# Cosine attention ahead of a leaky-ReLU feed-forward: one PSUM store, score tiles in blocks of three, squares behind norm products, weights requested at other places

## Chip, cores and metric

The kernel runs on one core of a Trainium2 chip. The metric is device time of one execution in microseconds; lower is better. A core has five engines with instruction streams of their own: TensorE (PE, with weight loads shown apart as PEld), VectorE (DVE), ScalarE (ACT), GpSimd (POOL) and SyncE (SP). DMA requests are issued from SP, ACT and POOL and are carried by 16 DMA engines. Matrix products land in PSUM, which has 8 banks of 512 float32 columns on each of 128 partitions; SBUF is the larger working memory.

## What is computed

```python
def _attn_ref(q, k, v, tau):                 # 8 batches, 12 heads, 448 rows, 64 columns
    q_n = q / (np.linalg.norm(q, axis=-1, keepdims=True) + 1e-06)
    k_n = k / (np.linalg.norm(k, axis=-1, keepdims=True) + 1e-06)
    scores = np.matmul(q_n, k_n.transpose(0, 1, 3, 2)) / tau
    scores = scores - np.max(scores, axis=-1, keepdims=True)
    attn = np.exp(scores)
    attn = attn / (np.sum(attn, axis=-1, keepdims=True) + 1e-09)
    return np.matmul(attn, v).astype(np.float32)

def _moe_ref(x, w_in, w_out):                # 3584 rows, 768 -> 2048 -> 768
    h = x @ w_in
    g = np.maximum(0.01 * h, h)
    return (g @ w_out).astype(np.float32)
```

`x` is the attention's output with the heads side by side: 3584 rows (8 batches of 448) of 768 columns.

## The kernel before

**Slots.** Two heads of one batch form a slot `s`: 6 slots a batch (NPAIR), 48 in all. Two slots form a quad `j` of four heads: 3 a batch (NQ), 24 in all.

**Loads.** `load_qk(s)` issues four DMA requests on SP (q rows 0 to 383, k rows 0 to 383, and the last 64 rows of q and of k); four buffers, so slot s+4 is requested once slot s is normalised. `load_v(j)` issues one request on POOL, `load_v_rem(b)` four. The weights come through POOL too: `load_w_in(i)`, four pieces of 768 KB, `load_w_out(half)`, two of 1536 KB. POOL takes its instructions in order, so a request stands behind whatever POOL does before it.

**Norms of a slot.** `squares(s)` (L141: POOL, two products, q and k; the first three slots partly on ACT and DVE), `sums(s)` (L152: DVE, two reduces), `roots(s)` (L159 to L161: ACT, logarithm, exponential, addition), `normalise(s)` (L169 reciprocal and L173, the two "norm products" `qn`, DVE). `transposes(s)` then makes `qkT[s]`: up to slot 9 on TensorE with a DVE copy out of PSUM (L187, L208), from slot 10 on as a DMA transpose on SP (L202). `norms(s)` is roots, normalise, the DMA transpose and the loads of slot s+4. `hold(x)` is a copy of one column on POOL that reads `x`: what stands behind it on POOL does not start before `x` is written.

**Scores.** `scores(s, kis)` makes key tiles: for tile 0, 1 or 2 two matmuls of 64 contraction rows, side by side in the array (64x128, one for each head); tile 3 holds the last 64 keys of both slots of a quad and takes four matmuls of 64x64. Each key tile fills two PSUM banks, and one ACT exponential of 128x896 empties it (L238). All matmuls of one call are issued first, then its exponentials.

**Attention of a quad.** `totals(j)` sums the exponentials with a matrix of ones (16 matmuls of 128x32, four abreast) and takes the reciprocal on ACT as logarithm and exponential (L260, L261). `products(j, e)` multiplies with v (16 such matmuls for each of two halves `e`), `scale(j, e)` (L279, DVE) multiplies the result out of PSUM with the reciprocal into `xT`. `attend(j)` is all of it: 48 matmuls, 2 ACT, 2 DVE instructions. The text calls it the attention.

**Feed-forward.** Eight chunks `c` of 384 or 512 rows in turn. `first(c, m)`: 16 groups of 6 matmuls against w_in, each emptied by ACT as a leaky ReLU (L301, Prelu). `second(c, ts, half)`: groups of 16 matmuls against w_out, each emptied by a DVE copy (L331), then stored by SP. `work` lists the groups with a due place; `feed(place)` issues those that are due, `feed_groups(n)` the next n.

**PSUM.** Score tiles have a pool of two buffers of two banks (`p_sc`); all else (totals, values, transposes, both feed-forward products) rotates through four buffers of one bank (`p_mm`).

**Order.** The order of every engine is the order of the calls, written out by hand (`manual_schedule`). Opening: slots 0 to 5 in a loop (L440) with fill matmuls that keep TensorE busy. Then a stretch for slots 6 and 7, in which the first 13 w_in groups are issued. Then a loop over pairs of slots:

```python
        squares(s + 4)
        scores(s, (0, 1))
        attend(j)
        load_v(s // 2 + 1)
        scores(s, (2,))
        scores(s + 1, (0,))
        sums(s + 3)
        feed(s + 0.67)
        norms(s + 3)
        squares(s + 5)
        scores(s + 1, (1, 2))
        sums(s + 4)
        feed(s + 1.33)
        norms(s + 4)
        scores(s + 1, (3,))
        feed(s + 2)
```

In each batch's turn the chunk of the batch before is fed. After the last attention the rest of the feed-forward runs alone.

Of the kernel before, what the change touches and what calls it, by code (L numbers as in the profile page):

```python
# [8 lines left out]
F32 = mybir.dt.float32  # L9
# [7 lines left out]
def kernel(  # L17
# [27 lines left out]
    LATE = 0.3  # L45
    OPENING = 13
# [17 lines left out]
    scp = ctx.enter_context(tc.tile_pool(name="p_sc", bufs=2, space=PS))  # L64
    mmp = ctx.enter_context(tc.tile_pool(name="p_mm", bufs=4, space=PS))

    nc.scalar.preload_act_table_set("natural_log_exp_and_others")
    gp = nc.gpsimd

# [125 lines left out]

    def transposes(s):
        if s >= NSLOT:
            return
        dst = qtp.tile([128, 7, 128], BF16, name="qkT")
        qkT[s] = dst.rearrange("p t c -> p (t c)")  # L200
        if s >= DMA_FROM:
            nc.sync.dma_start(  # L202
                out=dst, in_=qn[s].rearrange("p t h d -> p (t h d)"), transpose=True
            )
            return
        tp = mmp.tile([128, 7, 128], BF16, name="tp", tag="mm")
        one(tp, s, 0, 7)
        nc.vector.tensor_copy(out=dst, in_=tp)  # L208
# [3 lines left out]
    def scores(s, kis):  # L212

        if s >= NSLOT:
            return
        tiles = []
        for ki in kis:
            sc = scp.tile([128, 2, 512], F32, name="sc")
# [11 lines left out]
        for ki, sc in zip(kis, tiles):  # L230
# [25 lines left out]
    def totals(j):  # L256
        sm = mmp.tile([128, 512], F32, name="sm", tag="mm")
# [8 lines left out]
    def products(j, e):  # L266
        b, jj = divmod(j, NQ)
        po = mmp.tile([128, 512], F32, name="po", tag="mm")
# [5 lines left out]
    def scale(j, e):  # L274
# [7 lines left out]
        )  # L282

# [5 lines left out]
    def first(c, m):  # L289
# [3 lines left out]
        pm = mmp.tile([128, 512], F32, name="pm", tag="mm")  # L293
# [22 lines left out]
    def second(c, ts, half):  # L316
        c0, n = chunk_cols(c)
        po2 = mmp.tile([128, 512], F32, name="po2", tag="mm")
# [29 lines left out]

    work = []
    for c in range(B):  # L350
        c0, n = chunk_cols(c)
        groups = [(6 * n, lambda c=c, m=m: first(c, m)) for m in range(MT)]
# [3 lines left out]
        groups += [  # L356
            (MT * HALF, lambda c=c, ts=ts, half=half: second(c, ts, half)) for ts, half in order
        ]
        total, done = sum(g[0] for g in groups), 0
        if c == 0:  # L360

            work += [(0, fn) for _, fn in groups[:OPENING]]
            groups = groups[OPENING:]
            total = sum(g[0] for g in groups)
        for cost, fn in groups:
            start = NPAIR * (c + 1) + (LATE if c else 2)
            end = NPAIR * (c + 2) + LATE
            work.append((start + (end - start) * (done + cost / 2) / total, fn))
            done += cost

    def feed(place):
        while work and work[0][0] <= place:
            work.pop(0)[1]()

    def feed_groups(count):
        for _ in range(count):
            work.pop(0)[1]()
# [23 lines left out]
    def fill(count):  # L401
        wm = mmp.tile([128, 512], F32, name="wm", tag="mm")
# [25 lines left out]
    for lo, hi, copy in ((0, 4, nc.scalar.copy), (4, 7, nc.vector.tensor_copy)):  # L428
        tp = mmp.tile([128, 7, 128], BF16, name="tp", tag="mm")
# [10 lines left out]
    for s in range(NPAIR):  # L440
# [16 lines left out]
        if s == 0:  # L457
            hold(qn[1][:, 6, 0, 0:1])
# [3 lines left out]
        if s < 4:  # L462
            load_w_in(s)
        if s == 4:
            load_w_out(0)
            load_v_rem(1)
# [19 lines left out]
    def attend(j):  # L486
        totals(j)
        for e in range(2):
            products(j, e)
# [10 lines left out]

    for s in range(NPAIR, NSLOT + 1, 2):
        j = s // 2 - 1
        if s == NPAIR:

            squares(s + 3)
            attend(j)
            scores(s, (0, 1))
            sums(s + 1)  # L510
            feed_groups(1)
            norms(s + 1)
            hold(qn[s + 1][:, 6, 0, 0:1])
            squares(s + 4)
            load_w_out(1)
            sums(s + 2)
            feed_groups(3)
            transposes(s + 1)
            roots(s + 2)
            feed_groups(2)  # L520
            scores(s, (2,))
            scores(s + 1, (0,))
            normalise(s + 2)
            load_qk(s + 6)
            hold(qn[s + 2][:, 6, 0, 0:1])
            load_v(s // 2 + 1)
            squares(s + 5)
            sums(s + 3)
            roots(s + 3)
            feed_groups(2)  # L530
            scores(s + 1, (1, 2))
            normalise(s + 3)
            load_qk(s + 7)
            feed_groups(1)
            transposes(s + 2)
            sums(s + 4)
            feed_groups(2)
            roots(s + 4)
            scores(s + 1, (3,))
            normalise(s + 4)  # L540
            transposes(s + 4)
            load_qk(s + 8)
            feed_groups(1)
            transposes(s + 3)
            feed_groups(1)
            continue
        squares(s + 4)
        scores(s, (0, 1))
        attend(j)
        if s >= NSLOT:  # L550
            break
        load_v(s // 2 + 1)
        scores(s, (2,))
        scores(s + 1, (0,))
        sums(s + 3)
        feed(s + 0.67)
        norms(s + 3)
        squares(s + 5)
        if (s + 2) % NPAIR == 0:
            load_v_rem(s // NPAIR + 1)  # L560
        scores(s + 1, (1, 2))
        sums(s + 4)
        feed(s + 1.33)
        norms(s + 4)
        scores(s + 1, (3,))
        feed(s + 2)
    feed(1e9)

# [34 lines left out]
```

## Time and profile before

| | us |
|---|---|
| median of 3 runs | 436.07 (435.71 to 436.48) |
| the profiled execution | 435.32 |
| its span, first to last instruction | 433.6 |
| granted TensorE clock over the span | 0.996 of full |
| TensorE busy, 0 to 42 us | 33.76 of 42.00 |
| TensorE busy, 61 to 382 us | 319.85 of 321.00 |
| one exponential of a score tile (L238) | 0.91 |
| one w_out request, issue to landing | 17.1 |
| one w_in request, issue to landing | 10.3 |

The profile was taken from one execution, and its times count from that execution's first instruction. A timeline line reads: start, length, engine, line of the code, operation, output and inputs by tile name, shape, number of instructions, and in brackets the idle time of the engine before it with what ended it. Matmul lengths overlap, since matmuls are pipelined and their ends are modelled; the step from one start to the next is the measured quantity. "128*32" behind a matmul is the part of the array in use, rows by columns.

### The profile page before, as it was taken

The page shows a single profiled execution, that of the slowest core. Times are in us where ns is not written, and L with a number is a line of the kernel's source. Part 1 is how long each engine was busy: PE and PEld are TensorE (multiplying, and loading weights), DVE is VectorE, ACT ScalarE, POOL GpSimd, SP SyncE. Part 2 cuts the span into 40 slices and gives each one's busy share as a digit, 9 for nine tenths or more (in the row PEclk, how much of TensorE's full clock was granted, in tenths as well). Part 3 has the DMA queues.
Part 4 walks back from the last instruction along what each step waited for, and adds up shares of the span by engine and source line. Part 5 has one row for each costly group of instructions (what it writes and reads, how often), then busy time and mean ns, then how long its engine had stood idle before and what let it go on. Part 6 is the DMA issues. An engine that isn't in the chain of part 4 may idle for free.

```text
span 433.6 us, 8498 instructions
## 1 busy us (share of the span) xinstructions
PE 418.9 (97%) x3305; PEld 206.0 (48%) x3319; DVE 189.3 (44%) x364; ACT 269.4 (62%) x496; POOL 129.6 (30%) x162
## 2 busy tenths in 40 slices
PE   8589999999999999999999999999999999999995
PEld 3134454544455555544455554544455555554563
DVE  5976755643335435632345444633436343220021
ACT  4897697488644788467753787557854587524300
POOL 4737642742161233341251213532232200000000
PEclk9999999999999999999999999999999999999999
DMA  8999999984468547766367555777185621010022
GB/s 169 187 223 255 212 219 183 167 200 114 82 115 178 109 113 141 135 142 140 45 149 142 125 136 105 129 178 143 23 173 119 101 58 23 36 74 2 0 74 73
DMA packets 104744, 54.11 MB, mean 125 GB/s; under 512 B 70784, under 2 KB 99712, under 8 KB 104704
## 3 DMA queue, kind: packets, MB, share of 16 engines
q1 hardware_dynamic: 79152, 41.44, 40.5%
q0 software_dynamic: 25056, 11.80, 22.0%
q8 instruction: 26, 0.43, 0.4%
q10 hardware_dynamic: 496, 0.33, 0.2%
q14 instruction: 14, 0.11, 0.1%
HBM read 45.61 MB, written 11.01 MB: 131 GB/s over the span
## 4 chain that ended last, share of the span: by engine, by line
PE 88%; DMA 6%; DVE 2%; ACT 1%; SPq 1%; issue 1%; POOL 0%; DVEq 0%; POOLq 0%
PE po L320 34%; PE pm L295 33%; PE sc L226 9%; PE po L249 8%; PE sm L249 4%; DMA q_h<-in_q_dram 4%; DVE qn L173 2%; DMA qkT<-qn 2%; ACT pe L238 1%; PE tp L187 0%; SPq L105 0%; SPq L102 0%; POOL sq L141 0%; DVE ss L152 0%; PE wm L404 0%
## 5 line engine op out<-in xcount | busy, mean ns | idle before, releaser
L238 ACT ACTIVATE pe<-sc 128x896 bf16<-128x896 f32 x144 | 123.6, 913 | 59.8 <-PE sc L226 57.3
L320 PE MATMUL po<-w_out_sb,hT 128*128 128x384 bf16 x896 | 151.9, 326 | 0.0
L295 PE MATMUL pm<-xT,w_in_sb 128*128 128x384 bf16 (+1 forms) x757 | 150.8, 352 | 0.9 <-issue 0.5
L320 PEld LDWEIGHTS <-hT 128*128 128x128 bf16 x896 | 84.8, 98 | 64.0 <-issue 10.4
L141 POOL TENSOR_TENSOR sq<-q_h 128x512 f32<-128x512 f32 x45 | 47.3, 1052 | 202.5 <-DMA q_h<-in_k_dram 153.5
L295 PEld LDWEIGHTS <-w_in_sb 128*128 128x128 bf16 x768 | 72.6, 98 | 74.1 <-issue 9.9
L301 ACT ACTIVATE hT<-pm 128x384 bf16<-128x384 f32 (+1 forms) x128 | 66.8, 545 | 51.5 <-PE pm L295 51.0
L331 DVE COPY osb<-po 128x384 f32<-128x384 f32 (+1 forms) x56 | 31.0, 554 | 91.6 <-PE po L320 87.5
L279 DVE TENSOR_TENSOR xT<-po,rb 128x448 bf16<-128x448 f32 x48 | 27.9, 619 | 70.6 <-ACT rb L261 70.6
L152 DVE TENSOR_REDUCE ss<-sq 128x8 f32<-128x512 f32 (+1 forms) x96 | 55.2, 610 | 2.1 <-ACT sq L139 1.1
L226 PE MATMUL sc<-qkT 64*128 64x448 bf16 (+1 forms) x384 | 50.5, 362 | 4.1 <-ACT pe L238 2.4
L169 DVE RECIPROCAL r<-ss 128x14 f32<-128x14 f32 x48 | 11.5, 239 | 66.7 <-ACT ss L161 66.7
L141 POOL TENSOR_TENSOR sq<-k_h 128x384 f32<-128x384 f32 x45 | 38.7, 859 | 0.0
L173 DVE TENSOR_TENSOR qn<-q_h,r 128x512 bf16<-128x512 f32 x48 | 36.0, 750 | 1.9 <-DVE r L169 0.3
L249 PE MATMUL po<-pe,v_b 128*32 128x448 bf16 x576 | 35.6, 353 | 0.0
L226 PEld LDWEIGHTS <-qkT 64*128 64x128 bf16 (+1 forms) x384 | 11.8, 96 | 40.6 <-issue 36.3
L173 DVE TENSOR_TENSOR qn<-k_h,r 128x384 bf16<-128x384 f32 x48 | 29.4, 612 | 0.0
L159 ACT ACTIVATE ss<-ss,tiny 128x14 f32<-128x14 f32 x48 | 14.6, 305 | 14.9 <-DVE ss L152 14.9
L238 ACT ACTIVATE pr<-sc 128x896 bf16<-128x896 f32 x24 | 21.7, 903 | 1.5 <-PE sc L226 1.5
L249 PEld LDWEIGHTS <-v_b 128*32 128x32 bf16 x576 | 15.2, 97 | 11.9 <-issue 0.4
L128 POOL DMA_DIRECT2D v_rem<-in_v_dram x32 | 20.4, 642 | 0.0
L120 POOL DMA_DIRECT2D v_b<-in_v_dram x24 | 19.3, 805 | 0.0
(39 smaller groups left out, 161.2 us busy)
## 6 DMA issues: line engine op xcount, KB each, us to landing
q_h<-in_q_dram SPq DMA_DIRECT2D x48, 192.0 KB, 3.2
k_h<-in_k_dram SPq DMA_DIRECT2D x47, 192.0 KB, 3.2
out_dram<-osb SPq DMA_DIRECT2D x30, 192.0 KB, 2.8
v_b<-in_v_dram POOLq DMA_DIRECT2D x24, 192.0 KB, 3.9
out_dram<-osb SPq DMA_DIRECT2D x12, 384.0 KB, 2.9
w_in_sb<-in_moe_w_in_dram POOLq DMA_DIRECT2D x4, 768.0 KB, 10.3
w_out_sb<-in_moe_w_out_dram POOLq DMA_DIRECT2D x2, 1536.0 KB, 17.1
q_h<-in_q_dram SPq DMA_DIRECT2D x48, 32.0 KB, 3.2
```

Of the source, the lines that this page charges most:

```text
L128: gp.dma_start(out=vrb[b % 2][lo : lo + 64, :, g], in_=r[g])
L141: eng.tensor_tensor(sq, x, x, op=ALU.mult)
L152: nc.vector.tensor_reduce(o.rearrange("p (h t) -> p h t", h=2), sqs[s][i], axis=AX.X, op=ALU.add)
L173: nc.vector.tensor_tensor(qn[s][:, lo:hi], x.rearrange("p h t d -> p t h d"), r[:, r0 : r0 + 2 * nt].rearrange("p (h t) -> p t h", h=2) .u ...
L226: nc.tensor.matmul(out=out[:, a, :S], lhsT=x[rows, c0:c1], rhs=x[rows, 0:S], start=True, stop=True,)
L238: nc.scalar.activation(out=dst, in_=sc[:, :, :S], func=AF.Exp, scale=inv_tau)
L249: nc.tensor.matmul(out=x[32 * g : 32 * g + 32, :S], lhsT=weights(g, ki) if ki < 3 else rem(g), rhs=pe[s][:, ki, a, :] if ki < 3 else pr[j] ...
L279: nc.vector.tensor_tensor(xT[m][:, 2 * jj + e, half * S : (half + 1) * S], pos.pop((j, e))[:, :S], rbs[j], op=ALU.mult,)
L295: nc.tensor.matmul(out=pm[:, :n], lhsT=w_in_sb[:, kt, m * 128 : (m + 1) * 128], rhs=xT[c // 2][:, kt, c0 : c0 + n], start=(kt == 0), stop= ...
L301: nc.scalar.activation(out=hT[c][:, m, :n], in_=pm[:, :n], func=AF.Prelu, alpha=0.01)
L320: nc.tensor.matmul(out=po2[:, :HALF], lhsT=hT[c][:, m, ts * 128 : (ts + 1) * 128], rhs=w_out_sb[:, m, half * HALF : (half + 1) * HALF], st ...
L331: nc.vector.tensor_copy(out=o[:, half * HALF : half * HALF + cut], in_=po2[:, :cut])
```

## The change

Five things are changed.

1. The two PSUM pools become one tile `ps` of all eight banks. `banks(count)` hands out one bank, or two that start at an even bank, those that were used longest ago; `kept` keeps value banks of the opening out of it until they are scaled. In the opening (`deals["apart"]`) two-bank tiles come from banks 0 to 3 and single ones from 4 to 7, afterwards all from all.
2. From batch 1 on, the loop over pairs of slots becomes a list of units: seven a batch (`whole`), five in batch 1 (`opened`). A unit is an optional attention, then a block of two or three key tiles (all their matmuls, then all their exponentials), then sums, norms, hold and the next squares for the slot `ahead`, then a share of the feed-forward groups. The attention, where there is one, stands directly ahead of the block, no longer between two pairs of key tiles. A 64x64 tile is the last of its block.
3. The share of a unit is worked out from the columns of the groups that are left, with a weight for an attention (ATTEND) and for a block (BLOCK); one group is left over for the next batch and is issued first there.
4. A `hold` on the norm products stands ahead of every `squares` on POOL from slot 3 on: the squares of slot s+1 start after the norm products of slot s (in the opening and up to slot 9: those of slot s+2).
5. The four w_in pieces are requested in the opening's slots 0, 2, 3 and 4, where they were in 0 to 3; v's remainders of batch 1 in slot 5 (was 4); both halves of w_out in the stretch for slots 6 and 7, the first behind `norms` of slot 7, the second behind the squares of slot 10 and the load of v.

```diff
-    scp = ctx.enter_context(tc.tile_pool(name="p_sc", bufs=2, space=PS))
-    mmp = ctx.enter_context(tc.tile_pool(name="p_mm", bufs=4, space=PS))
+    psp = ctx.enter_context(tc.tile_pool(name="psum", bufs=1, space=PS))
...
+    ps = psp.tile([128, 8, 512], F32, name="ps")
+    age = [0] * 8
+    kept = {}
+    deals = {"n": 0, "apart": True}
+
+    def banks(count, keep=None):
+        lo, hi = (0, 8) if not deals["apart"] else (0, 4) if count == 2 else (4, 8)
+        x = min(
+            (i for i in range(lo, hi, count) if not set(range(i, i + count)) & set(kept.values())),
+            key=lambda i: max(age[i : i + count]),
+        )
+        deals["n"] += 1
+        age[x : x + count] = [deals["n"]] * count
+        if keep:
+            kept[keep] = x
+        return ps[:, x] if count == 1 else ps[:, x : x + count]
...
     def scores(s, kis):
-        if s >= NSLOT:
-            return
+        key_tiles([(s, ki) for ki in kis])
+
+    def key_tiles(which):
         tiles = []
-        for ki in kis:
-            sc = scp.tile([128, 2, 512], F32, name="sc")
+        for s, ki in which:
+            sc = banks(2)
...
-        if s == 0:
-            hold(qn[1][:, 6, 0, 0:1])
+        hold(qn[s + 1][:, 6, 0, 0:1])
         squares(s + 3)
         if not even:
             load_v(s // 2 + 1)
-        if s < 4:
-            load_w_in(s)
-        if s == 4:
-            load_w_out(0)
+        if s != 1 and s < 5:
+            load_w_in(max(s - 1, 0))
+        if s == 5:
             load_v_rem(1)
...
     def attend(j):
         totals(j)
+        po = banks(2)
         for e in range(2):
-            products(j, e)
+            products(j, e, po[:, e])
         for e in range(2):
             scale(j, e)
...
+    deals["apart"] = False
+    s, j = NPAIR, NQ - 1
+    attend(j)
+    scores(s, (0, 1))
+    sums(s + 1)
+    feed_groups(0, 1)
+    norms(s + 1)
+    load_w_out(0)
+    hold(qn[s + 1][:, 6, 0, 0:1])
+    squares(s + 3)
...
+    hold(qn[s + 2][:, 6, 0, 0:1])
+    squares(s + 4)
+    load_v(s // 2 + 1)
+    load_w_out(1)
...
+    whole = [
+        (None, [(0, 0), (0, 1), (0, 2)], 3),
+        (None, [(1, 0), (1, 1), (1, 2)], 4),
+        (None, [(2, 0), (2, 1), (1, 3)], 5),
+        (0, [(2, 2), (3, 0), (3, 1)], 6),
+        (None, [(3, 2), (4, 0), (3, 3)], 7),
+        (1, [(4, 1), (4, 2), (5, 0)], 8),
+        (None, [(5, 1), (5, 2), (5, 3)], None),
+    ]
+    opened = [
+        (0, [(2, 0), (2, 1), (2, 2)], 5),
+        (None, [(3, 0), (3, 1), (3, 2)], 6),
+        (None, [(4, 0), (4, 1), (3, 3)], 7),
+        (1, [(4, 2), (5, 0), (5, 1)], 8),
+        (None, [(5, 2), (5, 3)], None),
+    ]
+    queue = []
+    for b in range(1, B):
+        queue += work[b - 1]
+        units = opened if b == 1 else whole
+        costs = [BLOCK + (ATTEND if at is not None else 0) for at, _, _ in units[1:] + [(2, 0, 0)]]
+        for i, (at, tiles, ahead) in enumerate(units):
+            share = (sum(g[0] for g in queue[:-1]) + sum(costs[i:])) / (len(units) - i) - costs[i]
+            if b > 1 and i == 0:
+                at = -1
+            if at is not None:
+                attend(b * NQ + at)
+                load_v(b * NQ + at + 2)
+            key_tiles([(b * NPAIR + p, ki) for p, ki in tiles])
+            if ahead and b * NPAIR + ahead < NSLOT:
+                s = b * NPAIR + ahead
+                sums(s)
+                norms(s)
+                hold(qn[s][:, 6, 0, 0:1])
+                squares(s + 1)
+            if at == 1:
+                load_v_rem(b + 1)
+            done = 0
+            while len(queue) > 1 and (i == len(units) - 1 or done + queue[0][0] / 2 <= share):
+                cost, fn = queue.pop(0)
+                fn()
+                done += cost
+    attend(B * NQ - 1)
+    for cost, fn in queue + work[B - 1]:
+        fn()
```

## The prediction

> **What bounds the kernel now.** First the page: busy time and the chain that ended last.
>
> ```profile
> PE 418.9 (97%) x3305; PEld 206.0 (48%) x3319; DVE 189.3 (44%) x364; ACT 269.4 (62%) x496; POOL 129.6 (30%) x162
> ...
> PE 88%; DMA 6%; DVE 2%; ACT 1%; SPq 1%; issue 1%; POOL 0%; DVEq 0%; POOLq 0%
> ```
>
> TensorE sets the end; the 12% that is not its own must lie somewhere, and the windows put it early: of the first 42.0 us TensorE is busy 33.76, of 61 to 382 us 319.85 of 321. So two questions: what in TensorE's solid stretch is not matrix work, and what it waits for in the opening. For the first, TensorE's timeline of one pair of slots (start, length, instructions):
>
> ```profile
> 121.34 0.55 PE L226 MATMUL sc<-qkT 64*128 64x448 bf16 x4
> 121.83 0.75 PE L249 MATMUL sm<-pe,ones 128*32 128x448 bf16 x12
> ...
> 124.21 0.55 PE L226 MATMUL sc<-qkT 64*128 64x448 bf16 x4
> 124.70 5.37 PE L320 MATMUL po<-w_out_sb,hT 128*128 128x384 bf16 x32
> 130.00 0.55 PE L226 MATMUL sc<-qkT 64*128 64x448 bf16 x4
> 130.49 2.77 PE L320 MATMUL po<-w_out_sb,hT 128*128 128x384 bf16 x16
> 133.19 0.38 PE L226 MATMUL sc<-qkT 64*64 64x448 bf16 x4
> ```
>
> Read starts, not lengths. 32 matmuls take 5.30 (124.70 to 130.00), 16 take 2.70: the second 16 cost 2.60, so 0.10 of each stretch is the change of array shape at its end. A score block holds two waves; a wave of 448 columns is 0.19 (48 strip matmuls, four abreast, are 12 waves in 2.38 less 0.10), so 0.49 - 0.38 = 0.11 is again the change. A pair of slots has eight changes: about 0.105 each, 0.84 us.
>
> For the opening, three timelines over the same time, TensorE, VectorE, GpSimd:
>
> ```profile
> 17.90 0.40 PE L187 MATMUL tp<-id,qn 128*128 128x128 bf16 x4 [0.89 <-DVE qn L173]
> 19.21 0.34 PE L187 MATMUL tp<-id,qn 128*128 128x128 bf16 x3 [0.91 <-DVE qn L173]
> ...
> 32.42 0.81 PE L187 MATMUL tp<-id,qn 128*128 128x128 bf16 x7 [0.87 <-DVE qn L173]
> 15.54 2.30 DVE L173 TENSOR_TENSOR qn<-q_h,r 128x512 bf16<-128x512 f32 x1
> 17.76 1.39 DVE L173 TENSOR_TENSOR qn<-k_h,r 128x384 bf16<-128x384 f32 x1
> ...
> 34.53 0.69 DVE L173 TENSOR_TENSOR qn<-q_h,r 128x512 bf16<-128x512 f32 x1
> ...
> 35.61 0.62 DVE L279 TENSOR_TENSOR xT<-po,rb 128x448 bf16<-128x448 f32 x1
> 16.21 1.05 POOL L141 TENSOR_TENSOR sq<-q_h 128x512 f32<-128x512 f32 x1
> 17.21 1.31 POOL L141 TENSOR_TENSOR sq<-k_h 128x384 f32<-128x384 f32 x1
> ...
> 35.47 1.11 POOL L141 TENSOR_TENSOR sq<-q_h 128x512 f32<-128x512 f32 x1 [2.42 <-DMA q_h<-in_k_dram]
> ```
>
> The norm products (L173) take 0.69 and 0.55 alone, 2.30 and 1.39 while GpSimd squares: lost is about the time of overlap. L279, one input of which is in PSUM, keeps 0.62 under a square. TensorE's transposes wait for the slowed ones.
>
> **The change, part by part.** *Squares held.* The hold copy (0.18) puts slot s+3's squares behind slot s+1's products. Slot 2's products then take 1.24 from 15.54, ready 16.8 for 19.15. Next comes: reduce 0.54, transposes, copy 0.62, so slot 2's scores start at 18.35 for 20.27: 1.9 gained. ScalarE allows it: its exponentials end at 18.16, with roots (0.8) at 19.0, and its first exponential of slot 2 was at 20.87. Slot 3's key product (1.18 at 21.60, squares beside it) gives 0.6 more: 2.5. Behind the hold on GpSimd stand the squares, then v and weight requests; who waits is the next reduce. Squares take 1.87, ending about 2.2 after the products; a slot of the opening lasts 4.7: covered.
>
> *w_in later.* The 0.87 at 32.42: slot 5's reciprocal stood behind slot 6's reduce on VectorE, that behind squares at 29.73, these behind a load issued from 17.90 to 20.91 that landed at 29.56, beside w_in requests of 15.38, 19.27 and 22.31. Now only the first of these is in flight, and the load goes out 2 us earlier: +0.9. Opening 3.4; bounds 1 (this term alone) and 4.2 (every idle stretch before a product). Slot 7 repeats the story: idle of 0.25 and 0.87 at 45.5 to 47.0 before its transposes, products 0.99 and 1.18: 0.9 gained (0 to 1.1). The last w_in piece goes out near 32.4 and lands some 10 to 12 later, before the ninth w_in group (49).
>
> *Blocks of three.* Counted in the built order from the first w_in matmul on, changes of shape fall from 169 to 143: 26 x 0.105 = 2.7 gained. Of the 143, twenty go from 64x128 straight to 64x64, which no row shows: between nothing and 0.11. The nearest row, where the column tile alone changes (128x128 to 128x32 at 382.50), costs 0.11, so I charge them in full; free, they give 2.1 more. About 14 more waves inside blocks at 0.01 each cost 0.15.
> On this the Trainium skill (TensorEngine Tiling, Key Properties) speaks against the joining: a change of mode, not of tile, drains the array. By it the gain is the 26; were the column tile no mode, 46, 4.8 us.
>
> *One PSUM store, attention ahead.* Attention (totals, then both halves of values) now precedes its scores. One row of before shows that order, the last attention:
>
> ```profile
> 382.50 0.75 PE L249 MATMUL sm<-pe,ones 128*32 128x448 bf16 x12
> 383.49 0.54 ACT L260 ACTIVATE rb<-sm 128x448 f32<-128x448 f32 x1 [2.66 <-PE sm L249]
> ...
> 384.68 1.16 DVE L279 TENSOR_TENSOR xT<-po,rb 128x448 bf16<-128x448 f32 x2 [1.51 <-ACT rb L261]
> 384.88 2.77 PE L320 MATMUL po<-w_out_sb,hT 128*128 128x384 bf16 x16
> ```
>
> Nine banks are wanted and eight exist: totals 1, values 2, scores 6. The built waits go by bank: the third score tile takes the totals' bank (free after L260, 1.53 after the start, wanted at 2.8), and the first feed-forward group takes the first value bank. That one is free when the first scaling ends, 2.80 after the start; the score block puts the group at 2.39 + 0.40 + 0.28 = 3.07. Margin 0.27, no cost, if ScalarE is free at 0.99. ScalarE's queue before it: three exponentials at 0.81 (two take 1.73, the next starts 1.61 later) are 2.43, roots 0.8, the leaky ReLUs 0.38 each back to back. Tightest is a 384-column chunk's third unit: 2.43 + 0.8 + 3 x 0.38 = 4.4 from 0.5 after its start, against 3.9 to the next attention plus 0.99: even. I charge 0.3 (0 to 20 attentions x 0.17 = 3.5). VectorE and the held squares have slack: squares end about 7.4 after a unit's start, units last 6.8, and the reduces are wanted only at 2.9 of the next. Loads and SP's transposes keep their distance of a slot or more.
> Against this stands the skill (TensorEngine Tiling, PSUM Bottleneck): tiling speeds TensorE, not the emptying of PSUM. The rows agree in kind (0.19 a tile written, 0.81 emptied); by the rule alone the case is the slower rival below.
>
> *Where it changes over.* In the first unit after slot 7 the third tile waits for two leaky ReLUs behind three exponentials and roots: 7.0 against 6.6, costs 0.4, once. Slot 10's DMA transpose is asked near 53.5; the one in the trace took 59.10 to 69.78 under the second w_out load. It is wanted near 66.4, and w_out, later on GpSimd too, lands near 67: I charge 0.5 (0 to 2). Slot 11's transpose, which held TensorE 0.5 at 73.96, is now asked near 61.5, lands by 68.4 with its 6.84 of before, and is wanted near 72.5: 0.5 gained. The tail is the same.
>
> Sum: 433.6 - 3.4 - 0.9 - 0.5 - 2.7 + 0.15 + 0.3 + 0.4 + 0.5 = 427.45. The profiled run took 435.32, 1.72 around its span: 429.2; the shown median, 436.07, is 0.75 over that run: 429.9, say 430.
>
> **The rivals.** *The opening keeps its length.* If ScalarE or the loads set its pace, 3.4 + 0.9 are lost: 434.2. For it: ScalarE runs without a gap from 11.64 to 18.16. Against: its roots of 19.65 had waited 1.49 for VectorE's reduce, which stood behind the slowed products. *The inner change is free:* 430 - 2.1 = 427.9, more with an opening at its upper bound: 426. *Slower: ScalarE, first in first out, reaches the totals late.* Place: all 20 attentions. Each 0.1 over the margin of 0.27 costs 2 us; it turns the sign when the logarithm is 0.27 + 6.1 / 20 = 0.58 late. One exponential ahead of it (0.81) gives 20 x 0.54 = 10.8: 441. For it: the even balance above. Against: that holds in three chunks' one unit; elsewhere TensorE's units outlast ScalarE's share of them (6.6 against 5.5, 9.7 against 6.0). *The store does not divide:* if a wait meant the whole tile, every group would wait for every bank, far over 441; the built waits name single banks, so I count it with the slower case.
>
> **How the numbers follow.** Forecast, 427 to 433: 0.60. Inner change free, under 427: 0.10. Opening keeps its length, 433 to 435.2: 0.12. Within 0.2% (about what this kernel's measurement can tell from no change): 0.04. Slower: 0.14. Faster is then 0.82. The range 425.5 to 435.5 leaves about 0.2 out, most of it above.
>
> **What would show it.** Right: norm products of 0.69 and 0.55 everywhere, no idle of 0.9 before transposes at 17 and 19, the first w_in matmul near 38.4; scores of six matmuls followed by a group 0.68 later; 64x64 matmuls 0.29 after the last 64x128 pair started. Wrong: idle before w_in or w_out groups right behind score blocks, released by the scaling of the values or by a leaky ReLU; a first w_in matmul still near 41.8; a wait for a DMA transpose of several microseconds near 66.

## The result and the profile after

| | us |
|---|---|
| before, median of 6 runs | 436.37 |
| after, median of 6 runs | 432.23 (432.1 to 434.12) |
| ratio | 0.9909, 95% interval 0.9888 to 0.9931 |
| profiled execution, span | 432.51, 430.5 (before 435.32, 433.6) |

The forecast was 430, range 425.5 to 435.5: faster, as forecast, by some two thirds of what was forecast. The changed kernel was run once more as the control of the experiments: 434.05 (432.06 to 434.19), ratio 0.9938 (0.9918 to 0.9958), so there by about two fifths. Its executions gather at 432.1 and at 434.1, five of six near the lower in the first set, four of six near the upper in the control.

First the page of the changed kernel: busy time, and the chain that ended last, by engine and by line.

```profile
PE 415.6 (97%) x3305; PEld 207.8 (48%) x3319; DVE 187.1 (43%) x364; ACT 268.6 (62%) x496; POOL 136.1 (32%) x205
...
PE 91%; DMA 5%; ACT 2%; DVE 1%; issue 1%; SPq 0%; DVEq 0%; ACTq 0%
PE ps L324 34%; PE ps L349 33%; PE ps L275 13%; PE ps L252 9%; DMA qkT<-qn 3%; DMA q_h<-in_q_dram 1%; PE ps L417 1%; DMA q_h<-in_k_dram 1%; PE ps L209 1%; ACT pe L264 1%; SPq L127 0%; DVE qn L195 0%; ACT sq L161 0%; ACT pr L264 0%; DVE xT L306 0%
```

VectorE's share of the chain fell from 2% to 1%: the norm products are off it. But the DMA transposes (`qkT<-qn`) rose from 2% to 3%. Where that lies is found by cutting the span at matmuls that every kernel has: the first score matmul, the first against w_in, the first against w_out, the first of chunk 1 against w_in, the last one. Their starts are in TensorE's timelines; the differences, in us:

| stretch | before | after | control | after less before |
|---|---|---|---|---|
| start to first score matmul | 10.31 | 10.37 | 10.43 | +0.06 |
| to the first w_in matmul ("opening") | 31.47 | 28.97 | 29.33 | -2.50 |
| to the first w_out matmul | 23.59 | 22.98 | 23.84 | -0.61 |
| to chunk 1's first w_in matmul | 24.47 | 26.70 | 27.08 | +2.23 |
| to the last matmul ("steady stretch") | 339.01 | 336.72 | 336.72 | -2.29 |
| to the end | 4.71 | 4.78 | 4.79 | +0.07 |

The opening's gain is there, and two rows later most of it is gone (2.23 of 3.05). What is left at the end is mostly the steady stretch. TensorE's timeline of the changed kernel in the third and fourth row, then SP's queue:

```profile
68.44 0.86 PE L252 MATMUL ps<-qkT 64*128 64x448 bf16 x8 [0.76 <-DMA qkT<-qn]
...
74.33 0.36 PE L252 MATMUL ps<-qkT 64*128 64x448 bf16 x2
76.83 0.55 PE L252 MATMUL ps<-qkT 64*128 64x448 bf16 x4 [2.14 <-DMA qkT<-qn]
77.32 2.77 PE L349 MATMUL ps<-w_out_sb,hT 128*128 128x384 bf16 x16
...
56.47 1.35 SPq L227 DMA_TRANSPOSE qkT<-qn  x1
...
62.75 5.97 SPq L227 DMA_TRANSPOSE qkT<-qn  x1
```

The kernel before at the same place, SP's queue and TensorE:

```profile
67.79 1.26 SPq L202 DMA_TRANSPOSE qkT<-qn  x1
...
73.96 0.36 PE L226 MATMUL sc<-qkT 64*128 64x448 bf16 x2
74.67 0.36 PE L226 MATMUL sc<-qkT 64*128 64x448 bf16 x2 [0.35 <-DMA qkT<-qn]
```

By starts, TensorE loses 0.83 to slot 10's transpose (from the first w_out matmul, 62.31, to 68.44 is 6.13, where 32 such matmuls and the change take 5.30) and 2.31 to slot 11's (74.33 to 76.83 is 2.50 for a wave of 0.19). Before, slot 11's cost 0.52 (73.96 to 74.67) and slot 10's nothing. Slot 10's was asked at 56.47 and landed at 68.40. Slot 11's reached SP at 62.75, stayed there for 5.97, and landed at 76.79, 14.0 after it was asked. The answer for w_out's requests in the changed kernel has the last line

```profile
DMA to landing us min/median/max: 20.7/22.5/24.3
```

(17.1 was the median before). With that, w_out's second half, asked at 50.35, landed at 74.6; before, asked at 51.91, it landed at 69.6.

The opening, TensorE and VectorE:

```profile
15.64 0.69 DVE L195 TENSOR_TENSOR qn<-q_h,r 128x512 bf16<-128x512 f32 x1
16.25 0.55 DVE L195 TENSOR_TENSOR qn<-k_h,r 128x384 bf16<-128x384 f32 x1
...
16.76 1.03 PE L417 MATMUL ps<-warm 128*128 128x512 bf16 x2
17.72 0.59 PE L252 MATMUL ps<-qkT 64*64 64x448 bf16 x4
18.25 0.56 PE L209 MATMUL ps<-id,qn 128*128 128x128 bf16 x7
18.65 0.59 PE L417 MATMUL ps<-warm 128*128 128x512 bf16 x2
19.53 0.55 PE L252 MATMUL ps<-qkT 64*128 64x448 bf16 x4 [0.29 <-ACT ss L181]
```

Norm products of 0.69 and 0.55, done at 16.80, as forecast. But the transposes begin at 18.25 with no idle time ahead of them: TensorE itself was late. Two fill matmuls took 1.03 at 16.76, and 0.59 at 18.65. The windows say why; columns after the span are its length, TensorE's busy time and count, granted clock, DMA share (packet times added up over 16 engines, so that it can pass 1), GB/s. The changed kernel:

```profile
14.00:16.00 2.00, 1.04 (x5) 0.71 0.75 212
16.00:18.00 2.00, 2.00 (x9) 0.50 0.48 58
18.00:20.00 2.00, 1.71 (x17) 0.93 1.10 194
```

and the kernel before:

```profile
16.00:18.00 2.00, 1.11 (x10) 1.00 0.57 56
...
20.00:22.00 2.00, 1.73 (x6) 0.55 1.05 215
22.00:24.00 2.00, 2.00 (x22) 0.60 1.32 232
```

Both kernels lose about 1.7 us of clock there, 2 x (0.29 + 0.50 + 0.07) and 2 x (0.45 + 0.40). In the changed one that lies ahead of slot 2's transposes, where the holds were to save time, in the one before behind them.

The steady stretch, TensorE around one attention of the changed kernel:

```profile
124.90 0.74 PE L275 MATMUL ps<-pe,v_b 128*32 128x448 bf16 x12
125.46 0.36 PE L275 MATMUL ps<-pr,v_rem 128*32 128x448 bf16 x4
125.76 0.74 PE L252 MATMUL ps<-qkT 64*128 64x448 bf16 x6
126.43 5.37 PE L349 MATMUL ps<-w_out_sb,hT 128*128 128x384 bf16 x32
131.74 0.86 PE L252 MATMUL ps<-qkT 64*128 64x448 bf16 x8
```

Six score matmuls straight behind the values, a group 0.67 later (125.76 to 126.43), no bracket anywhere: the forecast's picture. TensorE's list of waits in this profile names no scaling of values and no leaky ReLU.

### The profile page after: what moved, and what is told of

It is laid out like the page before. It is cut to its first block, busy times and chain, and to the rows that moved or that the text cites. A ratio compares the mean times of both kernels' runs of the same rounds, so it can differ in the third digit from the quotient of the medians.

```text
span 430.5 us, 8622 instructions
## 1 busy us (share of the span) xinstructions
PE 415.6 (97%) x3305; PEld 207.8 (48%) x3319; DVE 187.1 (43%) x364; ACT 268.6 (62%) x496; POOL 136.1 (32%) x205
## 4 chain that ended last, share of the span: by engine, by line
PE 91%; DMA 5%; ACT 2%; DVE 1%; issue 1%; SPq 0%; DVEq 0%; ACTq 0%
PE ps L324 34%; PE ps L349 33%; PE ps L275 13%; PE ps L252 9%; DMA qkT<-qn 3%; DMA q_h<-in_q_dram 1%; PE ps L417 1%; DMA q_h<-in_k_dram 1%; PE ps L209 1%; ACT pe L264 1%; SPq L127 0%; DVE qn L195 0%; ACT sq L161 0%; ACT pr L264 0%; DVE xT L306 0%
## 5 line engine op out<-in xcount | busy, mean ns | idle before, releaser
L264 ACT ACTIVATE pe<-ps 128x896 bf16<-128x896 f32 x144 | 122.6, 917 | 50.1 <-PE ps L252 49.2
L349 PE MATMUL ps<-w_out_sb,hT 128*128 128x384 bf16 x896 | 151.8, 326 | 0.0
L324 PE MATMUL ps<-xT,w_in_sb 128*128 128x384 bf16 (+1 forms) x757 | 150.2, 352 | 0.6
L330 ACT ACTIVATE hT<-ps 128x384 bf16<-128x384 f32 (+1 forms) x128 | 65.0, 540 | 40.2 <-PE ps L324 39.7
L360 DVE COPY osb<-ps 128x384 f32<-128x384 f32 (+1 forms) x56 | 30.8, 552 | 97.2 <-PE ps L349 90.7
L174 DVE TENSOR_REDUCE ss<-sq 128x8 f32<-128x512 f32 (+1 forms) x96 | 56.8, 613 | 19.6 <-POOL sq L163 16.8
L252 PE MATMUL ps<-qkT 64*128 64x448 bf16 (+1 forms) x384 | 47.3, 363 | 6.4 <-DMA qkT<-qn 2.9
L306 DVE TENSOR_TENSOR xT<-ps,rb 128x448 bf16<-128x448 f32 x48 | 27.9, 619 | 29.3 <-ACT rb L287 29.2
L275 PE MATMUL ps<-pe,v_b 128*32 128x448 bf16 x576 | 35.6, 353 | 0.0
L286 ACT ACTIVATE rb<-ps 128x448 f32<-128x448 f32 x24 | 13.0, 543 | 35.3 <-PE ps L275 35.3
L264 ACT ACTIVATE pr<-ps 128x896 bf16<-128x896 f32 x24 | 22.2, 926 | 0.6 <-PE ps L252 0.6
L275 PEld LDWEIGHTS <-v_b 128*32 128x32 bf16 x576 | 15.2, 97 | 11.9 <-issue 0.4
```

Source lines behind the costliest of these rows:

```text
L174: nc.vector.tensor_reduce(o.rearrange("p (h t) -> p h t", h=2), sqs[s][i], axis=AX.X, op=ALU.add)
L252: nc.tensor.matmul(out=out[:, a, :S], lhsT=x[rows, c0:c1], rhs=x[rows, 0:S], start=True, stop=True,)
L264: nc.scalar.activation(out=dst, in_=sc[:, :, :S], func=AF.Exp, scale=inv_tau)
L275: nc.tensor.matmul(out=x[32 * g : 32 * g + 32, :S], lhsT=weights(g, ki) if ki < 3 else rem(g), rhs=pe[s][:, ki, a, :] if ki < 3 else pr[j] ...
L306: nc.vector.tensor_tensor(xT[m][:, 2 * jj + e, half * S : (half + 1) * S], pos.pop((j, e))[:, :S], rbs[j], op=ALU.mult,)
L324: nc.tensor.matmul(out=pm[:, :n], lhsT=w_in_sb[:, kt, m * 128 : (m + 1) * 128], rhs=xT[c // 2][:, kt, c0 : c0 + n], start=(kt == 0), stop= ...
```

## The experiments

All are compared with the kernel before on the same chip. A time without an interval is that of one execution. "Stretches" below are those of the table: opening, to w_out, to chunk 1, steady.

**The control.** No edit.

> The changed kernel again, as the control of its neighbours: 432.2 us, TensorE waiting 0.9 us near 67.4 and 2.3 us near 74.3 for the DMA transposes of slots 10 and 11.

434.05, 0.9938 (0.9918 to 0.9958). In its profile (434.19) one line of TensorE's timeline holds most of the waiting for loads:

```profile
78.52 0.55 PE L252 MATMUL ps<-qkT 64*128 64x448 bf16 x4 [3.21 <-DMA qkT<-qn]
```

w_out's halves landed at 63.6 and 78.3, slot 11's transpose at 78.5; slot 10's was not waited for, w_out's first half was, 0.31. This profile's span is 1.7 longer than the other's. Of that, 0.8 came from how late the weights landed (60.0 and 74.6 in the other), and slot 11's transpose beside them, 0.5 from a wait for a leaky ReLU at 51.2, and 0.4 lies up to the end of the opening; steady stretches are equal to 0.01.

**Requests for weights at their old places.**

```diff
-        if s != 1 and s < 5:
-            load_w_in(max(s - 1, 0))
-        if s == 5:
+        if s < 4:
+            load_w_in(s)
+        if s == 4:
+            load_w_out(0)
             load_v_rem(1)
...
     norms(s + 1)
-    load_w_out(0)
```

> The changed kernel with the requests for weights where they were before (w_in in slots 0 to 3, w_out's first half and v's remainders in slot 4). Theory 'shared line': the later requests pushed the end of the weights from 69.6 to 74.6 us, and the DMA transposes of slots 10 and 11 share the DMA engines with them; so w_out lands near 70 again, the two waits of TensorE fall from 3.2 us together to 0.6 or less, the opening loses at most the 0.9 us of the forecast, and the time is 429.8 to 431.0. Rival 'own pace': the transposes are late by their own place behind the loads of slots 8 to 11 on SP's queue; the waits stay near 3 us, the opening loses up to 0.9, and the time is 432.2 to 433.1.

433.08, 0.993 (0.9916 to 0.9944). Stretches 30.32, 26.03, 23.56, 336.72. Both waits for transposes are gone, and another stands in their place; TensorE:

```profile
60.13 0.75 PE L275 MATMUL ps<-pe,v_b 128*32 128x448 bf16 x12 [2.03 <-DMA v_b<-in_v_dram]
```

The v load of that attention now stands behind w_out's first half on GpSimd. Transposes: slot 10's landed at 69.7, slot 11's at 76.1, w_out's second half, asked only at 54.08, at 73.6. The time lies in the range of 'own pace' (432.2 to 433.1), but not for its reason, since the waits that it counted on are gone; 'shared line' missed the time. Against the control the total is the same within the intervals; the wait has another name.

**No holds in the opening.**

```diff
-        hold(qn[s + 1][:, 6, 0, 0:1])
+        if s == 0:
+            hold(qn[s + 1][:, 6, 0, 0:1])
         squares(s + 3)
```

> The changed kernel without the holds of the opening's slots 1 to 5 (slot 0 keeps its own; the holds after the opening stay). The forecast's term: norm products of 2.30 and 1.39 us beside squares again, the first w_in matmul 2.5 us later, near 41.8. Theory 'shared line': the DMA transposes do not move with TensorE, so the waits for slots 10 and 11 shrink from 3.2 to about 0.7 us, and the end moves by 0 to 0.9 us only: 432.2 to 433.1. Rival 'terms add up': the waits go along with TensorE and the end is later by the whole 2.5: 434.7.

430.87 (430.42 to 431.32, 4 runs), 0.9877 (0.9858 to 0.9895): faster than its control, and the fastest kernel of the study. Both theories missed the time, though the two waits shrank to 0.84 together, as 'shared line' had it. Stretches 29.80, 22.97, 24.64, 336.72: the opening is 0.5 to 0.8 longer than with the holds, and the stretch to chunk 1 is 2.1 to 2.4 shorter. TensorE:

```profile
68.77 0.86 PE L252 MATMUL ps<-qkT 64*128 64x448 bf16 x8 [0.29 <-DMA qkT<-qn]
...
75.57 0.55 PE L252 MATMUL ps<-qkT 64*128 64x448 bf16 x4 [0.55 <-DMA qkT<-qn]
```

Slot 11's transpose landed at 75.5, behind a second half of w_out that landed at 73.05. Ahead of that, w_in's second piece was requested at 21.11, before the first had landed (22.3). With the holds it went out at 23.64, after the first had landed (22.8), since it stands behind the held squares on GpSimd.

**Slots 10 and 11 transposed on TensorE.**

```diff
-    DMA_FROM = 10
+    DMA_FROM = 12
...
-    transposes(s + 4)
     load_qk(s + 8)
     feed_groups(0, 1)
     transposes(s + 3)
     feed_groups(0, 1)
+    transposes(s + 4)
...
+            if b == 1 and i == 0:
+                transposes(NPAIR + ahead)
```

> The changed kernel with slots 10 and 11 transposed on TensorE and copied by VectorE (DMA transposes from slot 12 on). Both waits for DMA transposes, 0.9 and 2.3 us, have nothing left to wait for; added are two times seven transposes at 0.81 us and a change of array shape of 0.1 each, 1.8 us: 430.8. If the waits are not the transposes' but some other wait that ends at the same time (a raw load, an exponential), TensorE still waits near 67 and 74 us and the time is 433 to 434. Slot 12 is then the first DMA transpose; it is asked near 72 us and wanted near 80.

432.06 (431.41 to 433.46), 0.9908 (0.9889 to 0.9928). No wait for a DMA transpose is left, the stretch to chunk 1 is 23.56, 3.1 less. The stretch to w_out is 26.00, 3.0 more:

```profile
56.53 0.40 PE L209 MATMUL ps<-id,qn 128*128 128x128 bf16 x4 [0.20 <-DVE qn L195]
57.63 0.34 PE L209 MATMUL ps<-id,qn 128*128 128x128 bf16 x3 [0.70 <-DVE qn L195]
...
65.09 0.81 PE L209 MATMUL ps<-id,qn 128*128 128x128 bf16 x7 [1.03 <-DVE qn L195]
```

Where I put them, TensorE comes 1.93 too early for the norm products. The 3.1 us were the transposes', then; the cure cost as much.

**Requests ahead of the holds.**

```diff
+        if not even:
+            load_v(s // 2 + 1)
+        if s != 1 and s < 5:
+            load_w_in(max(s - 1, 0))
+        if s == 5:
+            load_v_rem(1)
         hold(qn[s + 1][:, 6, 0, 0:1])
         squares(s + 3)
-        if not even:
...
```

> The changed kernel with all holds, but in the opening's slots the requests for v, w_in and v's remainders stand ahead of the hold on GpSimd, not behind it. Theory 'requests behind holds': a hold delays the request that stands behind it (w_in's second piece went out at 23.64 with holds, at 21.11 without), the DMA engines' backlog ends later, and with it the DMA transposes of slots 10 and 11. So the second piece goes out near 19, the last w_out piece lands at 70 to 73 (74.6 and 78.3 with the requests behind), the waits near 67 and 74 us shrink from 3.0 to 1.0 together, the opening keeps its 29 us from first score to first w_in matmul, and the time is 429.5 to 430.9. Rival 'the holds cost by themselves' (GpSimd's hold copies, reduces that come later): the waits stay at 2 us or more and the time is 432 or more.

432.65 (430.96 to 434.28, 5 runs), 0.9924 (0.9899 to 0.9949). There is no profile of this kernel to read. The edit did more than meant: w_in's first piece no longer has the hold of slot 0 ahead of it. In the last run below, which shares this edit, that piece went out at 8.12, before the raw loads of slot 3 had landed; in the changed kernel it was 15.47. So it decides nothing between the two theories.

**w_out's second half later, twice.** First behind slot 11's `norms`, then behind the squares that follow them:

```diff
     load_v(s // 2 + 1)
-    load_w_out(1)
...
                 norms(s)
+                if b == 1 and i == 0:
+                    load_w_out(1)        # first version
                 hold(qn[s][:, 6, 0, 0:1])
                 squares(s + 1)
+                if b == 1 and i == 0:
+                    load_w_out(1)        # second version
```

> The changed kernel with w_out's second half requested after the DMA transpose of slot 11 instead of ahead of slot 10's. Theory 'shared line': slots 10 and 11 no longer share the DMA engines with that half; slot 10's transpose, asked near 56.5, lands by 63 (was 68.4), slot 11's, asked near 62.7, lands by 69 (was 76.8), both waits are gone. w_out's second half then lands later, about 13 to 17 us after 62 to 65 us, and its first group, wanted near 75, waits 0 to 4 us. Rival 'own pace': slot 10's transpose still takes 10 us or more and slot 11's is still late.

433.93, 0.9945 (0.9924 to 0.9966). GpSimd had nothing to wait for there and sent the request at 56.62, 0.25 behind slot 10's transpose. That one still took 11.9, slot 11's 14.8. So being asked first does not help a transpose; whether company slows it, this run could not say.

> The changed kernel with w_out's second half requested behind the hold and squares that follow slot 11's norm products, so near 65 us (in the run with the request behind slot 11's norms only, GpSimd had not to wait for anything and sent it at 56.6). Theory 'shared line': from w_out's first half landing at 59 to 65 us nothing but loads is in flight beside the transposes, so slot 10's, asked near 56.5, lands by 65 instead of 68.3, slot 11's leaves SP by then and lands by 71 instead of 76 to 78, and TensorE's waits near 67 and 74 us are gone; w_out's second half lands at 77 to 80 and its first group, wanted near 75, waits 2 to 5 us: 431 to 434 in all. Rival 'own pace': slot 10's transpose still takes 11 us or more.

437.28, 1.0024 (1.0009 to 1.0039). Now the request went at 65.52. SP's queue, then TensorE:

```profile
57.39 1.34 SPq L227 DMA_TRANSPOSE qkT<-qn  x1
...
63.47 1.28 SPq L227 DMA_TRANSPOSE qkT<-qn  x1
...
81.05 4.85 PE L349 MATMUL ps<-w_out_sb,hT 128*128 128x384 bf16 x16 [6.09 <-DMA w_out_sb<-in_moe_w_out_dram]
```

and the landing times of the DMA transposes asked between 50 and 66 us, first in the changed kernel, then in this one:

```profile
DMA to landing us min/median/max: 11.9/13.0/14.0
```

```profile
DMA to landing us min/median/max: 4.7/6.0/7.3
```

Slot 10's landed in 7.3 (w_out's first half was in flight until 59.9), slot 11's in 4.7, both long before TensorE wanted them. This settles that the transposes were slow because of w_out beside them: theory "shared line". The price is w_out's: 6.09 of waiting for its second half. (The slots behind, asked while it was in flight, took 10.5 and 11.2.)

**The holds alone, in the kernel before.**

```diff
-        if s == 0:
-            hold(qn[1][:, 6, 0, 0:1])
+        hold(qn[s + 1][:, 6, 0, 0:1])
         squares(s + 3)
```

> The kernel before with the holds of the opening alone (slots 1 to 5), nothing else changed. The forecast's term: first w_in matmul 2.5 us earlier than 41.8. Theory 'the clock takes part of it': the norm products take 0.69 and 0.55, but the granted clock falls to half near 14 to 20 us in any case, TensorE comes to the transposes of slot 2 later than 17, and only 0.8 to 1.5 us of the 2.5 are left; with w_in's requests behind the holds and the DMA transposes where they were, the end is 0.5 to 1.5 us earlier: 434.9 to 435.9. Rival 'terms add up': 433.8.

436.40, 1.0003 (0.9991 to 1.0016): no change. Stretches 29.66, 25.17, 25.67, 339.01 against 31.47, 23.59, 24.47, 339.01. The opening gains 1.81; TensorE gives it back, and more (chunk 1's first w_in matmul is 0.7 later), mostly at three places:

```profile
59.24 0.76 PE L249 MATMUL po<-pe,v_b 128*32 128x448 bf16 x12 [1.40 <-DMA v_b<-in_v_dram]
73.11 0.75 PE L249 MATMUL po<-pe,v_b 128*32 128x448 bf16 x12 [1.09 <-DMA v_b<-in_v_dram]
75.38 0.36 PE L226 MATMUL sc<-qkT 64*128 64x448 bf16 x2 [0.27 <-DMA qkT<-qn]
```

**Blocks split.** One feed-forward group goes between the last score tile of a block and the ones ahead of it.

```diff
-            key_tiles([(b * NPAIR + p, ki) for p, ki in tiles])
+            key_tiles([(b * NPAIR + p, ki) for p, ki in tiles[:-1]])
+            done = 0
+            if len(queue) > 1:
+                cost, fn = queue.pop(0)
+                fn()
+                done += cost
+            key_tiles([(b * NPAIR + p, ki) for p, ki in tiles[-1:]])
```

> The changed kernel with one feed-forward group put between the second and the third score tile of each block of three (between the first and the second of a block of two). That adds two changes of array shape to a block, one where the last tile is a 64x64 one: 27 x 2 + 20 = 74 changes at most, x 0.105 = 7.8 us, 440 us. If changes cost nothing (the forecast's row was misread), 432; if only the wait for ScalarE counts, it is earlier than 432.

441.66. The steady stretch is 346.15, 9.43 longer. Counted in the trace, shape changes there rise from 119 to 177: 58 x 0.1 = 5.8. The rest is mostly a new wait, since the last tile's exponential now comes directly ahead of some totals. It comes eight times, six of them in this stretch, 0.53 each there by starts, 3.2 together; one of the two ahead of it:

```profile
83.63 0.37 PE L275 MATMUL ps<-pr,ones_rem 128*32 128x448 bf16 x4 [0.36 <-ACT pr L264]
```

So a block of three spares TensorE two things: the changes, and a wait for the last exponential.

**ScalarE later.** Two logarithms of the totals that nobody reads stand ahead of the real one.

```diff
         rb = rbp.tile([128, S], F32, name="rb")
+        if not deals["apart"]:
+            for _ in range(2):
+                nc.scalar.activation(late, sm[:, :S], func=AF.Ln)
```

> The changed kernel with ScalarE's logarithm of the totals preceded by two more logarithms of the same totals that nobody reads (0.54 us each, 1.1 us together) in every attention after the opening. The forecast gave ScalarE a margin of 0.27 us there, past which each attention loses what it is late: 20 x (1.1 - 0.27) = 16.6, 449 us. If the margin is larger than 1.1 nothing happens: 432; in between, the loss of an attention tells the margin.

446.24. The steady stretch is 350.18, 13.46 longer; 17 of its attentions have a feed-forward group behind the score block, 0.79 each. The extra work delays the logarithm by 1.01, so 0.22 of it was margin. ScalarE, then TensorE:

```profile
125.43 1.12 ACT L288 ACTIVATE late<-ps 128x448 f32<-128x448 f32 x2 [3.38 <-PE ps L275]
126.44 0.54 ACT L289 ACTIVATE rb<-ps 128x448 f32<-128x448 f32 x1
...
126.82 0.74 PE L252 MATMUL ps<-qkT 64*128 64x448 bf16 x6
128.30 5.36 PE L352 MATMUL ps<-w_out_sb,hT 128*128 128x384 bf16 x32 [0.74 <-DVE xT L309]
```

The group behind the score block waits for the first scaling of the values (L309 here), the bank that the forecast named. The bracket on ScalarE, 3.38 idle, also tells why nothing of the kind happens by itself.

**The store divided.** The line `deals["apart"] = False` is left out.

> The changed kernel with the one store divided as in the opening to the end: two-bank tiles from banks 0 to 3, single ones from 4 to 7. The third score tile of a block then has to wait for the first one's exponential. It is wanted 0.8 us after the first tile's start and the exponential ends about 1.4 us after it: 0.6 us in each of some 46 blocks, and more where the values take two of the four banks: 28 us or more, 455 to 475 us in all. If the one store is not what lets the blocks of three run through, the time stays within 2 us of 432.

450.12. In program order a block's third tile is written over the first one before that is read, so the first tile's exponentials are taken of the third's scores; the wait that I expected in every block does not arise in that order, and the run is no measure of it. What it shows is another: TensorE stops between the first and the second tile behind an attention, since the second takes a bank pair that holds values.

```profile
128.34 0.81 PE L252 MATMUL ps<-qkT 64*128 64x448 bf16 x3
129.34 0.54 PE L252 MATMUL ps<-qkT 64*128 64x448 bf16 x3 [0.18 <-DVE xT L306]
```

Three waves and three more take 1.46 up to the next group instead of 0.67; the steady stretch is 15.5 longer.

**Neither holds nor requests behind squares.** The edit of the requests above, with the hold in slot 0 alone.

> The changed kernel without the holds of the opening's slots 1 to 5 and with each slot's requests for v, w_in and v's remainders ahead of its squares on GpSimd. Theory 'shared line': the weights form one queue that runs without a gap from its first request on, so that requests some 2 us earlier (13.6 for the first piece, 19 for the second) bring the last w_out piece in by 71 to 72 us (73.05 without holds, 74.6 and 78.3 with), slot 11's transpose by 74.5, and TensorE waits 0.3 us or less for both transposes: 429.7 to 430.5. Rival 'earlier weights slow the loads of the opening': raw loads of slots 4 to 7 land later, idle stretches ahead of the transposes of slots 5 and 7 return (0.87 each in the kernel before), 431 to 432.

435.31, 0.9974 (0.9958 to 0.999). w_in's first piece went out at 8.12, not 13.6. The opening is 35.76:

```profile
22.79 0.61 PE L209 MATMUL ps<-id,qn 128*128 128x128 bf16 x4 [3.06 <-DVE qn L195]
```

The last rows of slot 3's q and k landed at 16.8 and 18.3, beside w_in (18.1); in the changed kernel it was 13.3 and 13.5. The norms came that much later. The rival holds, for the opening, in a stronger form than written; how requests only 2 us earlier would do remains open.

## Why the prediction was right, and where it was not

**Shapes: right.** The fall from 169 changes to 143 was forecast at 2.7. The steady stretch has 23 of these 26 (142 before, 119 after) and is 2.29 shorter, 0.100 each; its length is the same to 0.01 in every profile whose units are unchanged, and it grew when changes were added ("Blocks split"). The unknown change, 64x128 to 64x64, measures 0.093 by starts, the median of 18: charging it in full was right, the rival "the inner change is free" falls, and with it the reading in which the column tile is no mode. The kinds of change, which the forecast had priced by one figure, range from 0.093 to 0.127 (64x64 to 128x128); the row that it read as 0.11 (128x128 to 128x32) is 0.094 by the same measure.

**ScalarE's margin: right, and the term too large.** Forecast 0.27, measured 0.22; the 0.3 charged for 20 attentions was not lost, since no attention was late. The slower rival's price (0.81 late, 20 x 0.54) is of the right kind: 1.01 late cost 0.79 each. It did not come up because ScalarE is idle ahead of the totals, 3.38 in the row under "ScalarE later".

**Slot 7, the first unit behind it: right.** No idle above 0.2 ahead of slot 7's transposes (0.25 and 0.87 before); the first unit's block took 0.45 more than a block elsewhere (61.18 to 62.31, 1.13 for 0.67), for 0.4. The stretch to the first w_out matmul is 0.61 shorter; the terms gave 0.5.

**The opening, 3.4: too large, in two ways.** Eight profiles share the same opening code: the granted clock over 10 to 42 us was 0.95 in four of them and the opening 28.95 to 29.33, it was 0.89 in the other four and the opening 29.70 to 31.62. The kernel before had 0.95 and 31.47. So at equal clock the gain is 2.1 to 2.5. First, the step "slot 2's scores start at 18.35" took TensorE as free at 17; at half clock it came at 18.25, and the scores at 19.53: 0.74 gained of 1.9. The Trainium skill (TensorE: Matmul & The Clock Gate, Part 1) states that the half clock is what TensorE gets by default and that activity lifts it; the trace agrees in that the drop, 0.50 at 16 to 18 us, follows 1.37 us of idle time ahead of 12.83, and TensorE had fewer than 1.1 us of work in each 2 us from 12 to 16. The kernel before had as little from 12 to 20 (1.01 to 1.14 in each 2 us) and kept 1.00 until 20, so the place of the drop does not follow from this alone. Second, 2.5 for the holds and 0.9 for w_in were added, and they overlap: with later requests and no holds the opening is 29.80 at 0.95; with the holds and the requests of before it is 29.66 in the kernel before and 30.32 in the changed one, both at 0.89, where the full change had 29.70 to 31.62. Either alone brings most of it.

**The changeover: the step that failed.** "Slot 11's transpose ... now asked near 61.5, lands by 68.4 with its 6.84 of before, and is wanted near 72.5: 0.5 gained", beside "w_out ... lands near 67". It was asked at 62.75, landed at 76.79 and cost 2.31 where before had 0.52: +1.8 for -0.5 (in the control it cost 3.4). Slot 10's, charged 0.5, cost 0.83, and w_out's second half, put near 67, landed at 74.6. I had taken durations over from the kernel before, though their size came from what shared the DMA engines. The windows of the kernel before show those engines with a busy share of 1.00 or more in every stretch of 8 us from 8 to 88 us. Requests on GpSimd's queue land one behind the other: in the changed kernel w_in's last piece at 44.1, v and its remainders by 47.9, w_out's first half at 60.0, v at 62.0, the second half at 74.6. So the last w_out stood at the end of a longer line, and the DMA transposes shared the engines with it. The run with that half held back shows it: 7.3 and 4.7 for 11.9 and 14.0. The half landed 5.0 later than before (74.6 for 69.6). By the landings, w_in's later end is 1.7 of these 5.0 (44.1 for 42.4); 2.0 is a v load that now stands ahead of that half, where before it stood behind it; the other 1.3 is that the same pieces took longer. The later requests for w_in are thus not the whole of it: with w_in at its old places the half still landed at 73.6, though asked 3.7 later. The Trainium skill (DMA: Bandwidth & Descriptors, Queues, rings and completion order) says that each DMA engine takes its queues in turn, a packet at a time; the runs agree, since asking the transpose 0.25 ahead of w_out's half did not help it, and its absence did.

**So the gain of the opening did not reach the end.** Start to chunk 1's first w_in matmul is 89.84 before, 89.02 after, 90.68 in the control, and 90.55 with the holds alone in the kernel before. This is the rival "the opening keeps its length" (434.2, chance 0.12) with another place: not ScalarE or the loads of the opening, but the weights some 40 us later. The rest, -2.29, is the shapes. The forecast's 430 counted on an opening whose gain the loads then took back. By stretches the sum missed at two places, 0.9 in the opening and 2.2 at the changeover, both the same way, so no error hid another; the range was wide enough to hold both. Two small figures are off too, neither of them in the sum: 20 x 0.17 is 3.4, not 3.5, and the free inner change with the opening at its upper bound comes to 427, not 426.

Without the holds of the opening the change gives 430.87, a ratio of 0.9877 (0.9858 to 0.9895) to the kernel before. What is seen in its profile is that w_out's second half and slot 11's transpose landed earlier there (73.05 and 75.5) than in the two profiles of the changed kernel (74.6 and 76.8, 78.3 and 78.5). But four other profiles with all the holds and the same requests for weights (TensorE transposes, store divided, blocks split, ScalarE later) have that half at 73.4 to 75.3, so most of this difference lies within what such profiles differ by. That the earlier request of w_in's second piece brings this is inferred from its time, and the two runs meant to test it moved the first piece as well. Why this kernel is the faster one stays open. A version with slots 10 and 11 on TensorE at a place where their norm products are ready was not tried.

## What to carry to other kernels

A stretch that runs ahead of a full transfer line can gain nothing at its end: before a saving is counted, find the next thing that TensorE waits for and ask whether it moves along. Take a transfer's duration from the old trace only if its neighbours on the DMA engines stay; otherwise add up what stands ahead of it on its queue. An instruction that waits on an engine which also issues DMAs delays every request behind it, and that may cost more than the collision that it avoids: here the kernel without the opening's holds was the faster one, though which wait decides it is not shown.

## What was not expected of the hardware

SP stayed on slot 11's DMA transpose for 5.97 us, until 0.3 after slot 10's had landed, and the loads behind it stayed with it; in the kernel before, with transposes 8.7 apart, it took 1.26. The next one, slot 12's, was held for 4.03, but left SP 0.8 before slot 11's landed, so the landing itself is not what it waits for. What it is stays open.

The clock lost in the opening is the same in the two profiles, but its place moved by some 5 us, from behind the place that the change was to speed up to just ahead of it. And it differs between executions of the same code, 0.95 or 0.89 over 10 to 42 us, with up to 2.7 us between the openings: a difference of 1 us there in a single pair of profiles says little.
